# Three-stage attention and mixing kernel: weight conversion taken off GpSimd, wider weight pieces, more result buffers

## The chip, the core and the metric

The kernel runs on one core of a Trainium2 chip. The metric is the device time of one execution in microseconds (us); lower is better. In the text PE is the matrix engine (TensorE), PEld its weight loads, DVE is VectorE, ACT is ScalarE, POOL is GpSimd, and SP is the engine that here only issues transfers (DMAs). ACT issues some transfers too.

## The reference, cut to what matters

The batch is 4, the sequence 768, the model width 512. An attention block (not touched) gives `x`. Two mixing blocks follow:

```python
# channel mixing: the end of block 2
y = yr + yi                       # token mixing with w_tok_r, w_tok_i
u = x + y
x = u + np.maximum(u @ w_ch, 0.0)
# gated block 3
h = gelu(x @ w_in)                # w_in is 512 x 1024: u is the first half, v the second
u, v = h[..., :512], h[..., 512:]
v_n = (v - mean(v)) / sqrt(var(v) + 1e-6) * g_ln
v_s = einsum('ts,bsd->btd', w_sg, v_n) + b_sg[None, :, None]
out = x + (u * v_s) @ w_out
```

Some inputs (`w_theta`, `w_ch`, `w_in`, `w_out` and the token weights) come in float64, `w_sg` in float32. The kernel keeps every weight as a pair of float32r tiles, high and low, and does each product as three matmuls (high*high, high*low, low*high).

## The kernel before, in words

**Stages.** PE walks through the program in a fixed order. First comes attention with the theta products (line 311, tile `th`) and the token mixing (line 378), up to 382.6 us of the profile. A theta product of one unit (12 matmuls) is followed by 24 matmuls of token mixing; `th` has one buffer in PSUM, and the next theta product can start when DVE's line 325 has read it. When a set of units is complete, DVE adds up `u` (lines 388, 389) and SP stores it to DRAM.

Then comes channel mixing, function `chan(c, e)`: 8 slices `c` of `u`, each with 4 groups `e` of 12 matmuls (line 432). DVE makes the result `x2e` of a group from PSUM (line 438), and SP stores it to DRAM. Each slice needs `uhi` (ACT) and `ulo` (DVE, line 113), which `split_u` makes from `uf`, loaded back from DRAM.

Then comes the gated stage, for each of four batch entries `b`: `h_v` (6 groups, line 514, with a gelu on ACT in line 520 that gives `gv`, and statistics on DVE), `rstd`, `h_u` (8 groups, line 552), `norm`, `v_s` (line 577), `final` (line 597). Only `b = 0` has weight conversions beside it.

PE's groups take their PSUM tile from four `acc` buffers: a group can start when the reader of the group four places before it is done.

**Weight conversion.** Class `Weights` loads a piece with a DMA into a `raw` buffer, and `convert` makes the two tiles from it. For a float64 piece the steps are: line 150 on ACT (`cvh`), lines 153, 156 and 160 on DVE (`cvh`, `cvm`), line 203 on ACT (the high tile), line 204 on DVE, then line 208 (`cvh` minus high) and line 209 (plus `cvm`: the low tile). Before the change lines 208 and 209 run on POOL for `w_ch`, `w_in` and `w_out`. A piece was 256 columns wide (256 KB) in `w_ch`, `w_in` and `w_out`, 384 columns in `w_sg`. `w_sg` is float32 and needs only a cast on ACT and a subtraction on DVE (both in line 112 or 113). The `raw` buffer of a float64 piece is free once DVE's line 204 has run.

`w_ch` is converted late in token mixing (from 319 us of the profile), `w_in` during channel mixing, `w_sg` and `w_out` around the end of channel mixing and in the first `h_v` and `h_u`. The loads of the gated stage's weights are issued by ACT, all other loads and stores in this part by SP.

**What sets the order.** The program is written with tile pools; a scheduler puts the instructions of each engine into one fixed order when the kernel is built, and each engine runs its own list strictly in that order. An instruction that waits holds up everything behind it on its engine.

Of the kernel before, what the change touches and what calls it, by code (L numbers as in the profile page):

```python
# [8 lines left out]
I32 = mybir.dt.int32  # L9
# [7 lines left out]
B, H, S, D = 4, 8, 768, 64  # L17
DM = H * D
# [14 lines left out]
def net_kernel(tc, qt, kw, vw, ident, w_theta, w_tok, w_ch, w_in, w_sg, w_out, g_ln, b_sg, out):  # L33
    nc = tc.nc

    def opened(name, bufs=1, **kw_):
        cm = tc.tile_pool(name=name, bufs=bufs, **kw_)
        return cm, cm.__enter__()

    NRAW = 3  # L40
    AO, CO = -4, -2
    NRAW1, NCV1 = 3, 2
    ZB = 2
# [71 lines left out]
    class Weights:  # L115
# [1 line left out]

        def __init__(self, pool, pieces, nraw, ncv=2, queue=None, raws=()):  # L120
            self.queue, self.raws = queue or nc.sync, raws
            self.pool, self.pieces, self.raw = pool, pieces, {}
            self.nraw, self.ncv = nraw, ncv
            self.n = max(p[0].shape[-1] for p in pieces if p[0].dtype != F32)

        def load(self, j):
# [17 lines left out]
        def bits(self, raw, n, scale, mag="act", rem="dve"):  # L144

            words = raw[:, 0:2 * n].rearrange("p (n t) -> p n t", t=2)
            low, high = words[:, :, 0], words[:, :, 1]
            h = self.pool.tile([128, self.n], I32, tag="cvh", name="cvh", bufs=self.ncv)[:, 0:n]
            m = self.pool.tile([128, self.n], I32, tag="cvm", name="cvm", bufs=self.ncv)[:, 0:n]
            nc.scalar.activation(  # L150
                out=h.bitcast(F32), in_=high.bitcast(F32), func=AF.Copy, scale=REBIAS
            )
            nc.vector.tensor_scalar(
                out=h, in0=h, scalar1=3, scalar2=None, op0=ALU.logical_shift_left
            )
# [239 lines left out]
    p2 = {}  # L395
# [50 lines left out]
    def open_w3():  # L446
        p3["w_cm"], w = opened("w3")
        p3["in_hi"] = [w.tile([128, KD, FF], F32R, name=f"in_hi{i}") for i in range(2)]
        p3["in_lo"] = [w.tile([128, KD, FF], F32R, name=f"in_lo{i}") for i in range(2)]
        p3["sg_hi"] = [w.tile([128, 2, S], F32R, name=f"sg_hi{i}") for i in range(3)]  # L450
        p3["sg_lo"] = [w.tile([128, 2, S], F32R, name=f"sg_lo{i}") for i in range(3)]
        p3["out_hi"] = w.tile([128, KD, DM], F32R, name="out_hi")
        p3["out_lo"] = w.tile([128, KD, DM], F32R, name="out_lo")
        p3["b"] = w.tile([128, S], F32, name="b_bc")
        p3["g"] = w.tile([128, KD], F32, name="g_col")
        open_x3()
        p3["s_cm"], stg3 = opened("stg3", bufs=2)
        pieces = []
        for j in (1, 0):
            for k in range(KD):  # L460
                for i, c in enumerate((slice(0, 256), slice(256, 512))):
                    pieces.append((
                        w_in[j, k, i], p3["in_hi"][j][:, k, c], p3["in_lo"][j][:, k, c]
                    ))
        for s in range(NBLK):
            for i, c in enumerate((slice(0, TC), slice(TC, S))):
                pieces.append((
                    w_sg[s, i],
                    p3["sg_hi"][s // 2][:, s % 2, c], p3["sg_lo"][s // 2][:, s % 2, c],
                ))  # L470
        for k in range(KD):
            for i, c in enumerate((slice(0, 256), slice(256, 512))):
                pieces.append((w_out[k, i], p3["out_hi"][:, k, c], p3["out_lo"][:, k, c]))
        p3["w"] = Weights(stg3, pieces, NRAW, 2, nc.scalar)
        nc.sync.dma_start(out=p3["b"], in_=b_sg.unsqueeze(0).to_broadcast([128, S]))
        nc.sync.dma_start(out=p3["g"], in_=g_ln)

# [127 lines left out]


    NU = len(units)
    half = dict(sub="pool", add="pool")
    P2, P3, P4 = [half], [dict(add="pool")], [half]
    NA = B * NBLK  # L610


# [32 lines left out]
    if True:  # L645
# [85 lines left out]
        for it in range(NU):  # L731
            run(it, -2)
            run(it, -1)
            for q in range(4):
                if has_theta(it + 2) and q == (3 if it < NBLK else 0):
                    theta(it + 2)
                run(it, q)
                if it >= 0:
                    mix_group(it, q)
                if it < CO + NFIRST and q == 3:  # L740
                    tok_conv()
                if last_att + 2 <= it < last_att + 6 and q % 2:
                    j = 2 * (it - last_att - 2) + q // 2
                    p2["w"].convert(j, **half)
                    p2["w"].load(j + NRAW)
                if has_theta(it + 2) and q == 3:
                    z_split(it + 2)
            run(it, 9)
            if it == NFIRST + CO - 1:
                close(st_cm)  # L750
                s1_cm, set1 = opened("set1")
                sets[1] = x_set(set1, 1, None)
            if it == last_att + 1:
                close(at_cm)
                close(s0_cm)
                open_p2()
                load_u(0)
                load_u(1)
                load_u(2)
            if it == last_att + 6:  # L760
                split_u(0)
        close(s1_cm)
        close(wk_cm)
        close(w1_cm)
        p2["x_cm"], p2["x"] = opened("p2x", bufs=2, side="right")
        open_w3()
# [25 lines left out]
        for b in range(B):  # L792
            for s in range(NBLK):
                h_v(b, s)
                if b == 0:
                    for _ in range(2):
                        w3s.convert(jw, **P3[jw % len(P3)])
                        w3s.load(jw + NRAW)
                        jw += 1
            rstd()  # L800
            for c in range(2):
                for f in range(KD):
                    h_u(b, c, f)
                    if b == 0:
                        w3s.convert(jw, **P4[jw % len(P4)])
                        w3s.load(jw + NRAW)
                        jw += 1
                    if c == 0:
                        norm(f)
                    elif f < 2:  # L810
                        norm(4 + f)
            if b == 0:
                close(p3["s_cm"])
            p3["xr"] = [x3_t.pop(2 * b), x3_t.pop(2 * b + 1)]
            if b + 1 < B:
                load_x2(2 * b + 2)
            for c in range(2):
                for f in range(KD):
                    v_s(b, c, f)
            if b + 1 < B:  # L820
                split_x2(2 * b + 2)
            for e in range(KD):
                final(b, 0, e)
            if b + 1 < B:
                load_x2(2 * b + 3)
                split_x2(2 * b + 3)
            for e in range(KD):
                final(b, 1, e)
# [4 lines left out]
def _layout(inp):  # L833
# [26 lines left out]
    def pieces(w, n):  # L860

        w = w.reshape(w.shape[0] // 128, 128, w.shape[1] // n, n).transpose(0, 2, 1, 3)
        return np.ascontiguousarray(w)
# [41 lines left out]
```

## Time and profile before

| | before |
|---|---|
| median of 3 runs | 769.97 us (769.75 to 771.89) |
| the profiled execution's own time | 770.49 us |
| its span in the profile | 768.7 us |
| PE busy | 732.5 us (95% of the span) |
| DVE busy | 495.0 us (64%) |
| ACT busy | 311.2 us (40%) |
| POOL busy | 61.3 us (8%), 64 of its 70 instructions are lines 208 and 209 |

Busy time is the union of an engine's instructions. Matmuls overlap on PE, so a matmul's duration in a row is longer than the distance from its start to the next one's. 1.8 us lie between the span and the execution's own time.

### The profile page before, as it was taken

Reading aid. Unit: us, or ns where it says so; the run is one execution under the profiler, and the core shown is the slowest. Engines: PE = TensorE matmul, PEld = TensorE weight load, DVE = VectorE, ACT = ScalarE, POOL = GpSimd, SP = SyncE. Lnnn points to the kernel's source line nnn. Section 1 sums busy time; section 2 is a strip of 40 time slices with the busy share of each in tenths; the row PEclk is TensorE's granted clock in tenths of the full one; section 3 lists DMA queues with packets and bytes.
Section 4 is the critical chain, followed back from the end, with each engine's and each line's share of the span. In section 5 each row is a group of like instructions: output and inputs, shape, how many; then the busy total and the mean of one; then the engine's idle time right before and its main releaser. Section 6 shows DMA issues by size and latency. Waiting matters only on the chain.

```text
span 768.7 us, 16388 instructions
## 1 busy us (share of the span) xinstructions
PE 732.5 (95%) x6968; PEld 680.8 (89%) x6968; DVE 495.0 (64%) x934; ACT 311.2 (40%) x500; POOL 61.3 (8%) x70
## 2 busy tenths in 40 slices
PE   5979999999999999989998899899999999999998
PEld 3757888999999999989997897899899989998998
DVE  5999898667476665896478958853355435543452
ACT  5965534545545545452124334711151125113310
POOL 0000000000000000160045614200000000000000
PEclk9998999999999999999999999999999999999999
DMA  9775376333233230521077865002100310030002
GB/s 343 283 236 176 134 227 193 111 99 129 95 126 123 84 128 2 205 71 42 28 248 255 285 194 152 10 1 103 62 1 1 109 57 1 1 113 10 1 1 83
DMA packets 35642, 86.92 MB, mean 113 GB/s; under 512 B 4081, under 2 KB 18033, under 8 KB 35569
## 3 DMA queue, kind: packets, MB, share of 16 engines
q1 hardware_dynamic: 30384, 77.22, 29.6%
q10 hardware_dynamic: 5184, 8.65, 4.0%
q8 instruction: 55, 0.90, 0.5%
q14 instruction: 19, 0.15, 0.1%
HBM read 66.98 MB, written 18.87 MB: 112 GB/s over the span
## 4 chain that ended last, share of the span: by engine, by line
PE 65%; DVE 18%; DMA 7%; ACT 6%; issue 3%; POOL 0%; SPq 0%; ACTq 0%; DVEq 0%; POOLq 0%
PE acc L378 16%; PE acc L577 13%; PE acc L597 9%; PE acc L552 8%; PE acc L514 7%; PE th L311 7%; PE att L234 3%; DVE cvh L156 2%; DVE cvm L204 2%; DMA raw<-w_sg 2%; DVE z L336 1%; DMA raw<-w_in 1%; DVE cvm L160 1%; PE att L258 1%; PE att L284 1%
## 5 line engine op out<-in xcount | busy, mean ns | idle before, releaser
L378 PE MATMUL acc<-tok,slot 128*128 128x384 f32 x552 | 116.9, 342 | 2.7 <-ACT slot L348 2.5
L378 PE MATMUL acc<-slot 128*128 128x384 f32 x552 | 115.6, 340 | 0.3 <-DVE u L388 0.3
L378 PEld LDWEIGHTS acc<-tok,slot 128*128 128x128 f32 x552 | 94.5, 188 | 5.2 <-ACT slot L348 2.8
L378 PEld LDWEIGHTS acc<-slot 128*128 128x128 f32 x552 | 95.5, 188 | 2.3 <-DVE u L388 0.6
L577 PE MATMUL acc<-sg_hi,vlo 128*128 128x384 f32 x192 | 64.4, 336 | 0.0
L577 PE MATMUL acc<-sg_hi,vhi 128*128 128x384 f32 x192 | 64.4, 336 | 0.0
L577 PE MATMUL acc<-sg_lo,vhi 128*128 128x384 f32 x192 | 64.4, 336 | 0.0
L311 PE MATMUL th<-th_hi,xhi 128*128 128x256 f32 (+1 forms) x168 | 53.1, 316 | 4.2 <-DVE slot_x L325 2.6
L112 ACT ACTIVATE ghi<-g 128x384 fp32r<-128x384 f32 x32 | 16.8, 525 | 87.7 <-DVE g L586 87.7
L311 PE MATMUL th<-th_hi,xlo 128*128 128x256 f32 (+1 forms) x168 | 51.6, 307 | 0.2 <-DVE xlo L113 0.2
L582 DVE SCALAR_TENSOR_TENSOR g<-acc,g_col,b_bc 128x384 f32<-128x384 f32 x32 | 19.8, 618 | 49.5 <-PE acc L577 49.5
L311 PE MATMUL th<-th_lo,xhi 128*128 128x256 f32 (+1 forms) x168 | 50.8, 302 | 0.0
L432 PE MATMUL acc<-uhi,ch_hi 128*128 128x384 f32 x128 | 44.7, 349 | 5.8 <-DVE x2e L438 5.6
L150 ACT ACTIVATE cvh<-raw 128x256 f32<-128x256 f32 (+1 forms) x44 | 24.8, 564 | 56.6 <-DMA raw<-w_in 19.9
L552 PE MATMUL acc<-x3hi,in_hi 128*128 128x384 f32 x128 | 43.2, 337 | 2.1 <-ACT gu L557 1.3
L432 PE MATMUL acc<-ulo,ch_hi 128*128 128x384 f32 x128 | 44.1, 344 | 0.5 <-DVE ulo L113 0.5
L432 PE MATMUL acc<-uhi,ch_lo 128*128 128x384 f32 x128 | 43.9, 343 | 0.0
L552 PE MATMUL acc<-x3lo,in_hi 128*128 128x384 f32 x128 | 43.0, 336 | 0.0
L552 PE MATMUL acc<-x3hi,in_lo 128*128 128x384 f32 x128 | 43.0, 336 | 0.0
L597 PE MATMUL acc<-glo,out_hi 128*128 128x384 f32 x128 | 43.0, 336 | 0.0
L597 PE MATMUL acc<-ghi,out_lo 128*128 128x384 f32 x128 | 42.9, 335 | 0.0
L597 PE MATMUL acc<-ghi,out_hi 128*128 128x384 f32 x128 | 42.9, 335 | 0.0
(141 smaller groups left out, 1627.5 us busy)
## 6 DMA issues: line engine op xcount, KB each, us to landing
va<-vw SPq DMA_DIRECT2D x24, 520.0 KB, 4.0
ka<-kw SPq DMA_DIRECT2D x24, 512.0 KB, 4.6
raw<-w_tok SPq DMA_DIRECT2D x12, 768.0 KB, 5.7
q<-qt SPq DMA_DIRECT2D x24, 256.0 KB, 3.0
u_dram<-u SPq DMA_DIRECT2D x32, 192.0 KB, 2.2
uf<-u_dram SPq DMA_DIRECT2D x8, 768.0 KB, 6.8
x_dram<-x2e SPq DMA_DIRECT2D x32, 192.0 KB, 3.3
x3f<-x_dram SPq DMA_DIRECT2D x8, 768.0 KB, 4.8
```

The source lines that it names most:

```text
L112: nc.scalar.activation(out=hi, in_=src, func=AF.Copy)
L150: nc.scalar.activation(out=h.bitcast(F32), in_=high.bitcast(F32), func=AF.Copy, scale=REBIAS)
L156: nc.vector.scalar_tensor_tensor(out=h, in0=high, scalar=-0x80000000, in1=h, op0=ALU.bitwise_and, op1=ALU.bitwise_or,)
L234: nc.tensor.matmul(out=out[32 * c:32 * c + 32, j, n * a:n * a + n], lhsT=lhs[h, a, 32 * c:32 * c + 32], rhs=rhs[h, 4 * a + c, :], start=Tr ...
L311: nc.tensor.matmul(out=th, lhsT=a[:, k, tok], rhs=w[:, k, cols], start=(i == 0), stop=(i == 3 * KD - 1),)
L378: nc.tensor.matmul(out=acc[:, 0:TC], lhsT=z[ri][:, zc], rhs=w[:, ri], start=(first and i == 0), stop=(last and i == 5),)
L432: nc.tensor.matmul(out=acc[:, 0:TC], lhsT=w[:, k, ee], rhs=x[:, k, :], start=(i == 0), stop=(i == 3 * KD - 1),)
L514: nc.tensor.matmul(out=acc, lhsT=x[:, k, tt], rhs=w[:, k, :], start=(i == 0), stop=(i == 3 * KD - 1),)
L552: nc.tensor.matmul(out=acc[:, 0:TC], lhsT=w[:, k, ff], rhs=x[:, k, :], start=(i == 0), stop=(i == 3 * KD - 1),)
L577: nc.tensor.matmul(out=acc[:, 0:TC], lhsT=v, rhs=w, start=(i == 0), stop=(i == 3 * NBLK - 1))
L582: nc.vector.scalar_tensor_tensor(out=g, in0=acc[:, 0:TC], scalar=p3["g"][:, f:f + 1], in1=p3["b"][:, tt], op0=ALU.mult, op1=ALU.add,)
L597: nc.tensor.matmul(out=acc[:, 0:TC], lhsT=w[:, k, ee], rhs=x[:, k, :], start=(i == 0), stop=(i == 3 * KD - 1),)
```

## The change

Three things are edited.

1. `w_ch`, `w_in` and `w_out` are converted with lines 208 and 209 on DVE in place of POOL.
2. The pieces of the gated stage's weights are twice as wide: `w_in` and `w_out` 512 columns (512 KB), `w_sg` 768 columns. There are half as many of them (8, 6 and 4), two `raw` buffers in place of three, and one `cvm` buffer in place of two. In `chan`'s loop a piece of `w_in` is converted at `e` 1 and 3 of the first two slices and at `e` 1 of the next four.
3. The pool of `x2e` has four buffers in place of two.

```diff
-    NRAW = 3
+    NRAW, NRAW3 = 3, 2
...
-            m = self.pool.tile([128, self.n], I32, tag="cvm", name="cvm", bufs=self.ncv)[:, 0:n]
+            m = self.pool.tile([128, self.n], I32, tag="cvm", name="cvm", bufs=self.ncm)[:, 0:n]
...
         for j in (1, 0):
             for k in range(KD):
-                for i, c in enumerate((slice(0, 256), slice(256, 512))):
-                    pieces.append((
-                        w_in[j, k, i], p3["in_hi"][j][:, k, c], p3["in_lo"][j][:, k, c]
-                    ))
+                pieces.append((w_in[j, k], p3["in_hi"][j][:, k], p3["in_lo"][j][:, k]))
...
-        p3["w"] = Weights(stg3, pieces, NRAW, 2, nc.scalar)
+        p3["w"] = Weights(stg3, pieces, NRAW3, 2, nc.scalar, ncm=1)
...
-    half = dict(sub="pool", add="pool")
-    P2, P3, P4 = [half], [dict(add="pool")], [half]
...
-                    p2["w"].convert(j, **half)
+                    p2["w"].convert(j)
...
-        p2["x_cm"], p2["x"] = opened("p2x", bufs=2, side="right")
+        p2["x_cm"], p2["x"] = opened("p2x", bufs=4, side="right")
...
-                if (e in (1, 3) or c < 2) and c < 7 and jw < 4 * KD:
-                    w3s.convert(jw, **P2[jw % len(P2)])
-                    w3s.load(jw + NRAW)
+                if (e == 1 or c < 2 and e == 3) and jw < 2 * KD:
+                    w3s.convert(jw)
+                    w3s.load(jw + NRAW3)
                     jw += 1
...
             for s in range(NBLK):
                 h_v(b, s)
                 if b == 0:
-                    for _ in range(2):
-                        w3s.convert(jw, **P3[jw % len(P3)])
-                        w3s.load(jw + NRAW)
-                        jw += 1
+                    w3s.convert(jw)
+                    w3s.load(jw + NRAW3)
+                    jw += 1
...
-                    if b == 0:
-                        w3s.convert(jw, **P4[jw % len(P4)])
-                        w3s.load(jw + NRAW)
+                    if b == 0 and f % 2:
+                        w3s.convert(jw)
+                        w3s.load(jw + NRAW3)
                         jw += 1
```

PE's list keeps its order. The lists of DVE and ACT change at three places that matter below.

**DVE late in token mixing.** The theta product here is `th_4435`, and `ulo_5091` (before) is the `ulo` of slice 1 of channel mixing. Before:

```order
L113 TENSOR_TENSOR ulo_4776<-uf_4429,uhi_4775 128x1536
L113 TENSOR_TENSOR slot_1875<-z_4385,slot_1875 128x512
L322 TENSOR_SCALAR slot_x_2018<-th_4435 128x256
L113 TENSOR_TENSOR ulo_5091<-uf_4431,uhi_5090 128x1536
L325 TENSOR_TENSOR slot_x_2018<-th_4435,slot_x_2018 128x256
```

With the change:

```order
L113 TENSOR_TENSOR ulo_4776<-uf_4429,uhi_4775 128x1536
L113 TENSOR_TENSOR slot_1875<-z_4385,slot_1875 128x512
L322 TENSOR_SCALAR slot_x_2018<-th_4435 128x256
L160 TENSOR_SCALAR cvm_4538<-cvh_4537 128x256
L325 TENSOR_TENSOR slot_x_2018<-th_4435,slot_x_2018 128x256
L204 SCALAR_TENSOR_TENSOR cvm_4538<-raw_4427,cvm_4538 128x256
L331 TENSOR_SCALAR z_4450<-slot_x_2018 128x256
L208 TENSOR_TENSOR cvh_4537<-cvh_4537,ch_hi_4421 128x256
```

The second `ulo` no longer stands between lines 322 and 325; it comes after line 325 of the next theta product, and lines 208 and 209 of `w_ch` are now in this list.

**DVE in channel mixing.** `x2e_5205` and `x2e_5237` are the results of groups 6 and 7 (of 0 to 31) before; `cvh_5180` is the sixth half-width piece of `w_in`. Before:

```order
L438 SCALAR_TENSOR_TENSOR x2e_5205<-acc_5192,uf_4431 128x384
L160 TENSOR_SCALAR cvm_5153<-cvh_5152 128x256
L204 SCALAR_TENSOR_TENSOR cvm_5153<-raw_5072,cvm_5153 128x256
L153 TENSOR_SCALAR cvh_5180<-cvh_5180 128x256
L156 SCALAR_TENSOR_TENSOR cvh_5180<-raw_5104,cvh_5180 128x256
L438 SCALAR_TENSOR_TENSOR x2e_5237<-acc_5224,uf_4431 128x384
```

With the change `x2e_5187` and `x2e_5217` are the results of groups 7 and 8, and `cvh_5142` and `cvh_5190` are the third and fourth full-width pieces:

```order
L438 SCALAR_TENSOR_TENSOR x2e_5187<-acc_5174,uf_4431 128x384
L160 TENSOR_SCALAR cvm_5143<-cvh_5142 128x512
L113 TENSOR_TENSOR ulo_5265<-uf_5108,uhi_5264 128x1536
L204 SCALAR_TENSOR_TENSOR cvm_5143<-raw_5058,cvm_5143 128x512
L208 TENSOR_TENSOR cvh_5142<-cvh_5142,in_hi1_4991 128x512
L153 TENSOR_SCALAR cvh_5190<-cvh_5190 128x512
L209 TENSOR_TENSOR in_lo1_4993<-cvh_5142,cvm_5143 128x512
L156 SCALAR_TENSOR_TENSOR cvh_5190<-raw_5106,cvh_5190 128x512
L438 SCALAR_TENSOR_TENSOR x2e_5217<-acc_5204,uf_4433 128x384
```

In both lists a line 153 that needs a piece's data stands ahead of a result that PE waits for; with the change it is a full-width piece, with lines 208 and 209 of the piece before it beside it.

**ACT at the start of the gated stage.** `gv0` is the gelu of the first `h_v` group; `raw_5923` and so on are pieces of `w_out`. Before:

```order
L112 ACTIVATE sg_hi2_4996<-raw_5919 128x384
L150 ACTIVATE cvh_5969<-raw_5923 128x256
L139 DMA raw_5947<-w_out 128x512
L150 ACTIVATE cvh_5998<-raw_5943 128x256
L203 ACTIVATE out_hi_5000<-cvh_5969 128x256
L139 DMA raw_5979<-w_out 128x512
L203 ACTIVATE out_hi_5000<-cvh_5998 128x256
L150 ACTIVATE cvh_6027<-raw_5947 128x256
L139 DMA raw_6008<-w_out 128x512
L520 ACT_TABLE_LOAD
L520 ACTIVATE gv0_5778<-acc_5805 128x512
```

With the change (line 512 is line 520 of before):

```order
L112 ACTIVATE sg_hi2_4996<-raw_5765 128x768
L112 ACTIVATE sg_hi2_4996<-raw_5785 128x768
L139 DMA raw_5805<-w_out 128x1024
L512 ACT_TABLE_LOAD
L512 ACTIVATE gv0_5680<-acc_5707 128x512
L139 DMA raw_5825<-w_out 128x1024
L512 ACTIVATE gv1_5681<-acc_5727 128x512
```

Three casts of `w_out` pieces and two of its high tiles no longer stand ahead of the first gelu.

## Rows read from the trace of the kernel before

**Rows 1.** Stretches: us; busy PE, PEld, DVE, ACT, POOL; PE clock; DMA share; GB/s.

```profile
316.00:382.60 66.60, 63.41 (x395) 62.12 (x394) 47.73 (x97) 24.00 (x48) 15.52 (x16) 1.00 0.25 86
382.60:460.50 77.90, 71.61 (x387) 68.95 (x386) 61.34 (x114) 27.80 (x49) 32.68 (x32) 0.96 0.75 244
460.50:498.40 37.90, 34.35 (x169) 30.10 (x169) 31.96 (x68) 22.43 (x43) 12.79 (x16) 1.00 0.31 87
540.00:573.50 33.50, 33.50 (x171) 30.23 (x170) 15.23 (x32) 14.16 (x23) 0.00 (x0) 1.00 0.09 32
```

**Rows 2.** PE's waits from 316 to 500 us: total, times, longest.

```profile
PE acc L432 <- DVE x2e L438: 5.6, 5, 2.2
PE th L311 <- DVE slot_x L325: 2.6, 2, 1.6
```

**Rows 3.** PE around a wait in channel mixing: start, duration, idle before.

```profile
405.18 0.33 PE L432 MATMUL acc<-uhi,ch_lo 128*128 128x384 f32 x1
405.35 0.34 PE L432 MATMUL acc<-ulo,ch_hi 128*128 128x384 f32 x1
407.60 0.44 PE L432 MATMUL acc<-uhi,ch_hi 128*128 128x384 f32 x1 [1.91 <-DVE x2e L438]
...
409.52 0.52 PE L432 MATMUL acc<-uhi,ch_hi 128*128 128x384 f32 x1
409.84 0.52 PE L432 MATMUL acc<-uhi,ch_lo 128*128 128x384 f32 x1
```

**Rows 4.** DVE at the same place.

```profile
406.32 0.29 DVE L153 TENSOR_SCALAR cvh<-cvh 128x256 int32<-128x256 int32 x1 [2.69 <-ACT cvh L150]
406.65 0.42 DVE L156 SCALAR_TENSOR_TENSOR cvh<-raw,cvh 128x256 int32<-128x256 int32 x1
406.99 0.55 DVE L438 SCALAR_TENSOR_TENSOR x2e<-acc,uf 128x384 f32<-128x384 f32 x1
```

**Rows 5.** The chain that ended last, at the same place: start, length, what.

```profile
399.57 6.21 DMA raw<-w_in
```

**Rows 6.** DMA issues of the whole span: KB each, median us to landing.

```profile
ka<-kw SPq DMA_DIRECT2D x24, 512.0 KB, 4.6
...
raw<-w_in ACTq DMA_DIRECT2D x16, 256.0 KB, 3.6
```

**Rows 7.** Instruction groups by shape: busy us, mean ns of one, idle before.

```profile
L156 DVE SCALAR_TENSOR_TENSOR cvh<-raw,cvh 128x256 int32<-128x256 int32 x32 | 19.9, 624 | 0.4
...
L208 POOL TENSOR_TENSOR cvh<-cvh,in_hi 128x256 f32<-128x256 f32 x16 | 18.0, 1129 | 66.2 <-ACT in_hi L203 50.4 <-DVE cvm L160 13.0 <-DVE cvh L153 1.7
...
L438 DVE SCALAR_TENSOR_TENSOR x2e<-acc,uf 128x384 f32<-128x384 f32 x32 | 17.4, 549 | 2.3 <-PE acc L432 1.3 <-DMA x_dram<-x2e 0.8
...
L113 DVE TENSOR_TENSOR vlo<-gv,vhi 128x512 fp32r<-128x512 f32 x24 | 15.5, 685 | 0.2 <-ACT vhi L112 0.2
...
L113 DVE TENSOR_TENSOR x3lo<-x3f,x3hi 128x1536 fp32r<-128x1536 f32 x8 | 14.0, 1755 | 2.4 <-ACT x3hi L112 2.4
...
L176 DVE SCALAR_TENSOR_TENSOR th_lo<-slot,cvm 128x512 fp32r<-128x512 uint32 x4 | 2.8, 690 | 0.1
L156 DVE SCALAR_TENSOR_TENSOR cvh<-slot,cvh 128x512 int32<-128x512 int32 x4 | 2.7, 687 | 0.1
L150 ACT ACTIVATE cvh<-slot 128x512 f32<-128x512 f32 x4 | 2.7, 671 | 5.1 <-DMA slot<-w_theta 5.0
...
L153 DVE TENSOR_SCALAR cvh<-cvh 128x512 int32<-128x512 int32 x4 | 1.7, 423 | 1.9 <-ACT cvh L150 1.8
```

**Rows 8.** DVE, then PE, at a wait in token mixing.

```profile
330.24 1.96 DVE L113 TENSOR_TENSOR ulo<-uf,uhi 128x1536 fp32r<-128x1536 f32 x1
...
332.58 0.38 PE L311 MATMUL th<-th_hi,xhi 128*128 128x256 f32 x1 [1.57 <-DVE slot_x L325]
```

**Rows 9.** ACT at the start of the gated stage.

```profile
464.09 0.52 ACT L112 ACTIVATE sg_hi<-raw 128x384 fp32r<-128x384 f32 x1 [1.00 <-DVE sg_lo L113]
...
471.38 1.28 ACT L520 ACT_TABLE_LOAD   x1 [0.39 <-ACT cvh L150]
```

More of the change, by code (lines that the diff above doesn't have):

```diff
@@ L115, in net_kernel, with __init__ @@
     class Weights:
-        def __init__(self, pool, pieces, nraw, ncv=2, queue=None, raws=()):
+        def __init__(self, pool, pieces, nraw, ncv=2, queue=None, raws=(), ncm=None):
             self.queue, self.raws = queue or nc.sync, raws
             self.pool, self.pieces, self.raw = pool, pieces, {}
-            self.nraw, self.ncv = nraw, ncv
+            self.nraw, self.ncv, self.ncm = nraw, ncv, ncm or ncv
             self.n = max(p[0].shape[-1] for p in pieces if p[0].dtype != F32)
@@ L460, in open_w3 @@
             for k in range(KD):
-                for i, c in enumerate((slice(0, 256), slice(256, 512))):
-                    pieces.append((
-                        w_in[j, k, i], p3["in_hi"][j][:, k, c], p3["in_lo"][j][:, k, c]
-                    ))
+                pieces.append((w_in[j, k], p3["in_hi"][j][:, k], p3["in_lo"][j][:, k]))
         for s in range(NBLK):
[L466 to L470, printed above, removed]
+            pieces.append((w_sg[s], p3["sg_hi"][s // 2][:, s % 2], p3["sg_lo"][s // 2][:, s % 2]))
         for k in range(KD):
-            for i, c in enumerate((slice(0, 256), slice(256, 512))):
-                pieces.append((w_out[k, i], p3["out_hi"][:, k, c], p3["out_lo"][:, k, c]))
-        p3["w"] = Weights(stg3, pieces, NRAW, 2, nc.scalar)
+            pieces.append((w_out[k], p3["out_hi"][:, k], p3["out_lo"][:, k]))
+        p3["w"] = Weights(stg3, pieces, NRAW3, 2, nc.scalar, ncm=1)
         nc.sync.dma_start(out=p3["b"], in_=b_sg.unsqueeze(0).to_broadcast([128, S]))
@@ L764, in net_kernel @@
         close(w1_cm)
-        p2["x_cm"], p2["x"] = opened("p2x", bufs=2, side="right")
+        p2["x_cm"], p2["x"] = opened("p2x", bufs=4, side="right")
         open_w3()
         w3s = p3["w"]
-        for j in range(NRAW):
+        for j in range(NRAW3):
             w3s.load(j)
@@ L875, in _layout @@
         "w_ch": pieces(inp["moe_w_ch"], 256),
-        "w_in": np.stack([pieces(w_in[:, :FF], 256), pieces(w_in[:, FF:], 256)]),
-        "w_sg": pieces(inp["moe2_w_sg"].T, TC),
-        "w_out": pieces(inp["moe2_w_out"], 256),
+        "w_in": np.stack([pieces(w_in[:, :FF], FF)[:, 0], pieces(w_in[:, FF:], FF)[:, 0]]),
+        "w_sg": pieces(inp["moe2_w_sg"].T, S)[:, 0],
+        "w_out": pieces(inp["moe2_w_out"], DM)[:, 0],
         "g_ln": np.ascontiguousarray(inp["moe2_g_ln"].reshape(KD, 128).T),
```

## The prediction

> **What bounds the kernel now.** I first read the busy shares of the page's head (the table above): PE is busy 95% of the span, so the end is set by PE's list and by the moments in which PE stands still. Since the change leaves PE's work alone, it can only win or lose such moments. Then I cut the span at the stages [rows 1]. In the second half of token mixing PE is idle 66.6 - 63.4 = 3.2 us. Channel mixing takes 77.9 us. Its 384 matmuls start 0.17 us apart when nothing stops them (405.18 and 405.35 in [rows 3]; over longer runs 0.1735), which is 66.6 us, so 11.3 us are lost there. The first `h_v` and `h_u` take 37.9 us, the same work for `b = 1` 33.5 us [rows 1], so 4.4 us are lost there. After it, and from `b = 1` on, PE has no gap. At most 3.2 + 11.3 + 4.4 = 18.9 us can be won.
>
> Then the waits. In channel mixing PE waits for `x2e` on DVE [rows 2]. The place at 407.60 shows how: PE stops for 1.91 us [rows 3]; DVE's line 438 that frees its PSUM tile starts at 406.99, right behind a line 153 that had stood still for 2.69 us because ACT's cast had no data [rows 4]; the data came by a transfer that took 6.21 us [rows 5], where the median is 3.6 [rows 6]. So it is not DVE's load alone: DVE waits in order for a weight piece while the result that PE needs stands behind it. The wait costs twice: at 409.52 the matmuls start 0.32 us apart, not 0.17 [rows 3]. The granted clock over the stage is 0.96 [rows 1]; if the rest of it ran at 2.4 GHz, some 6.2 us (2 x 0.04 x 77.9) ran at 1.2 GHz, in which about 19 matmuls fit and not 36: 2.9 us of the 11.3 are the clock after waits. I count 1.4 us for each of two long waits.
>
> **The change, part by part.**
>
> Lines 208 and 209 on DVE. The 64 POOL instructions go; the 1129 ns of one [rows 7] was latency inside a conversion, not on PE's path. What also goes is DVE's slowing beside POOL: line 156 took 0.42 us alone [rows 4] and 0.624 on average [rows 7]. What DVE gains: in token mixing 16 instructions of 256 columns at about 0.42 us (the price of line 156, which reads two SBUF tiles too), 6.7 us. Against it stand four lines for each of eight pieces that get back between 0 and 0.2 us each, 0 to 6.4. DVE is busy 47.7 of 66.6 us there [rows 1], so this may lie beside other work. What matters is the order: before, line 325 stood behind an `ulo` of 1.96 us, and PE waited 1.57 us at 332.58 [rows 8], 2.6 in two such places [rows 2]. After, line 325 follows line 160 at once; by durations it ends about 0.5 us before PE wants it at the first place, and about 1 us before at the next three. The last term of the 3.2 us, some 0.5 us around the `u` additions, stays. I take a gain of 2.5 us. Bounds: 2.7 won, or 1.5 lost if one 6.7 us lump lands before a line 325 with only that 0.5 us of room.
>
> Wide pieces in channel mixing. One piece costs DVE 0.42 + 0.69 + 0.42 + 0.69 + 2 x 0.685 = 3.6 us (lines 153, 156, 160 at line 153's price, 204 at line 176's, 208 and 209 at the price of `vlo`) [rows 7], less some 0.08 us for each overlap with the next. Two half pieces cost DVE 2 x (4 lines of 0.3 to 0.6), about the same, and then POOL. So DVE's total does not grow; the question is again what stands ahead of `x2e`.
>
> Count from the first matmul of channel mixing (time 0; group k is due at 2.08 k and needs the `x2e` of group k-4). Pieces 0 and 1 are issued at 2.5 as now, and land at 7 to 9. From line 153 of piece 0 (about 8.5) to the `x2e` of group 8 DVE has 4 lines 153, 4 of 156, 3 of 160, 3 of 204, 6 of 208 and 209, two `ulo` of 1.755 and six `x2e` of 0.55 [rows 7]: 18.7 us, less 27 overlaps of 0.08, makes 16.6: it would end at 25.1, just when group 12 is due (25.0). But line 153 of piece 3 must wait. Its buffer is free when line 204 of piece 1 has run (about 17), a 768 KB load of `x3f` is issued just before it, and it lands some 7 us later (a 512 KB load takes 4.6 [rows 6], a half piece with such loads ahead took 6.21 [rows 5]): 24. Then come the cast (0.67), line 153, line 209, line 156 and `x2e`: 26.9. PE stops for 1.9 us, and the clock costs 1.4. Piece 4 has the same fate: its load stands on ACT's list behind the `x3hi` cast, is issued at about 26.5, lands at 31.5, and the `x2e` of group 10 behind it ends at 34.6, when group 14 is due at 32.4: 2.2 us and 1.4 again. From piece 5 on fewer results stand between pieces, and DVE has room; I leave 1.1 us for late `ulo`. Sum 1.9 + 1.4 + 2.2 + 1.4 + 1.1 = 8.0 us lost, where 11.3 were: a gain of 3.3. Bounds: with all pieces in time nothing is lost (11.3 won); if pieces 2 to 7 each come 2 us later than I take, each stops PE for up to 2 us more: 12 more lost, 8.7 worse than now.
>
> A rule of the Trainium skill speaks to this. In the trace the half piece issued by ACT at 399.57 took 6.21 us [rows 5], as if it stood behind the larger loads on SP's queue. By the Trainium skill, "DMA: Bandwidth & Descriptors", section on queues, rings and completion order, each DMA engine takes turns between the queues that have work, packet by packet, so a small piece on ACT's queue should pass a large load on SP's. By that rule pieces 3 and 4 would land about 2 us earlier and both long waits would be gone, a total of about 755 us. The row fits it badly, so I do not sum by it.
>
> Four `x2e` buffers. DVE waited 0.8 us in all for the store of an old `x2e` [rows 7]; this goes, inside the 3.3 us.
>
> The gated stage's start. Before, the last high tile of `w_sg` was made at 464.09, and the table load ahead of the first gelu came at 471.38 [rows 9], 10.9 us after `h_v` began, held by `w_out` casts that waited for their loads. PE reaches the fifth `h_v` group after 4 x 12 matmuls of 0.234 us ((33.5 - 96 x 0.1735) / 72, with the 33.5 of [rows 1]), 11.2 us, and needs the first gelu by then. After, only the six `w_sg` pieces stand ahead. Six pieces in two buffers, about 6 us a pair (3.6 for the load, a cast and a subtraction of 768 columns of about 1 us each), begun about 9 us before channel mixing ends because only then are `raw` and ACT free, leave the gelu at about 5.5 us after its end: in time. `w_out` then goes between gelus; the last one may hold the eighth group for a few tenths. I take 0.6 of 4.4 us lost, a gain of 3.8 (bounds: 0.5 if every `w_sg` pair takes 4 us more and the gelu is as late as now, 4.4).
>
> Sum: 2.5 + 3.3 + 3.8 = 9.6 us. The profiled execution had 770.49 us; 770.49 - 9.6 = 760.9. The median of the runs is 0.5 us lower: 769.97 - 9.6 = 760.4 us. Changes under 0.3% (2.3 us) can't be told from none.
>
> **The rivals.**
>
> *Loads in time (0.18).* The waits for pieces 3 and 4 go, since wider loads need fewer turn-arounds. For: 3.6 us is the median for a piece [rows 6]. Against: the stage's DMA share of 0.75 [rows 1], which stays. Gain 2.5 + 7 to 11.3 + 4: 752 to 756 us.
>
> *The gain of channel mixing is eaten (0.20).* Pieces 3 to 6 stop PE as long as now, 11.3 us, and the clock with it; only the other two terms stay, one of them partly: 763.7 us, to 769 if both fall to half and channel mixing loses 2 more.
>
> *Two buffers are too few (0.09): slower.* With two buffers a pair of pieces costs a load of 7, a cast and 2.2 us of DVE, about 10 us, so pieces 2 to 7 take 30 us, and between their first and last lines stand the results of groups 6 to 20, 31 us of PE: just enough. If a pair took 17 us (a landing of 14), PE would be held to 51 us there: 20 lost, clock aside, for the 11.3 of now, against 6.3 won elsewhere: 772 us. It decides from a pair of about 16 us on. Against: no row near that size here.
>
> **How the numbers follow.** My forecast (756 to 763.5) gets 0.53, the rivals 0.18, 0.20 and 0.09. The range 752 to 768 leaves out the slower case, the worst of the second rival and the best of the first, about 0.2. Faster by over 0.3%: 0.53 + 0.18 + 0.12 of the second rival = 0.83. Within 0.3%: 0.09. Slower: 0.08.
>
> **What would show it.** Right: no POOL work beyond setup; line 156 at 0.69 us for 512 columns; no PE wait at line 311 for line 325 from 316 to 350; channel mixing in 72 to 76 us with one or two waits of about 2 us for `x2e`, behind a line 153 that waits for a piece, around groups 12 and 14, and the low clock after them; the first gelu some 6 us after `h_v` begins, `h_v` and `h_u` of `b = 0` in 34 us. Wrong: PE waits at other groups, or a channel mixing near 67 or above 78 us; DVE's instructions at 512 columns longer than 0.7 us; a new wait in token mixing.

## The result, and the profile after

The changed kernel takes 760.13 us (median of four executions, 757.85 to 762.43), the kernel before 770.12 (four, 769.75 to 771.89) beside it: a ratio of 0.986, with a 95% interval from 0.984 to 0.989, 10.0 us less. The prediction was 760.4. The profiled execution was the longest of the four, 762.43 us with a span of 760.6.

I cut the span at PE's first matmul of each stage. Ahead of them stands a fixed place that no edit touches, PE's wait at line 284 near 314 us; token mixing is counted from there. Lengths in us, with the change worked out:

| | before | after | change | predicted |
|---|---|---|---|---|
| up to the wait at line 284 | 313.60 | 315.30 | +1.7 | - |
| token mixing from there | 69.02 | 65.31 | -3.7 | -2.5 |
| channel mixing | 77.88 | 75.83 | -2.0 | -3.3 |
| `h_v` and `h_u` of `b = 0` | 37.94 | 33.75 | -4.2 | -3.8 |

The edited stages give 9.9 us; attention, which the change leaves alone, was 1.7 us longer in this execution. The stretches of the changed kernel that answer to [rows 1], the last 66.6 us of token mixing first, and two short ones inside channel mixing (the columns are those of [rows 1]):

```profile
314.00:380.60 66.60, 65.82 (x417) 65.21 (x416) 50.05 (x119) 24.30 (x49) 0.00 (x0) 1.00 0.26 92
380.60:456.44 75.84, 69.50 (x386) 67.98 (x385) 59.37 (x95) 25.01 (x28) 0.00 (x0) 0.98 0.75 255
456.44:490.19 33.75, 33.75 (x170) 30.49 (x169) 28.34 (x58) 21.49 (x34) 0.00 (x0) 1.00 0.28 88
414.00:424.00 10.00, 9.49 (x55) 9.17 (x55) 5.65 (x9) 1.56 (x3) 0.00 (x0) 1.00 0.98 335
...
430.00:440.00 10.00, 9.87 (x48) 9.87 (x49) 9.56 (x16) 3.53 (x4) 0.00 (x0) 0.83 0.59 198
```

POOL does nothing in them. The first `h_v` and `h_u` run without a gap, as `b = 1` did before. What is left of PE's waits from 316 to 500 us (total, times, longest), the answer to [rows 2]:

```profile
PE acc L432 <- DVE ulo L113: 4.1, 2, 3.6
PE acc L432 <- DVE x2e L438: 2.3, 2, 1.8
PE th L311 <- DVE slot_x L325: 0.3, 1, 0.3
```

The waits for `x2e` have shrunk from 5.6 us and a new one has come, for `ulo`. On PE (compare [rows 3]):

```profile
405.64 0.34 PE L432 MATMUL acc<-ulo,ch_hi 128*128 128x384 f32 x1
407.74 0.41 PE L432 MATMUL acc<-uhi,ch_hi 128*128 128x384 f32 x1 [1.76 <-DVE x2e L438]
407.99 0.34 PE L432 MATMUL acc<-uhi,ch_lo 128*128 128x384 f32 x1
...
426.22 0.34 PE L432 MATMUL acc<-uhi,ch_lo 128*128 128x384 f32 x1
430.13 0.54 PE L432 MATMUL acc<-ulo,ch_hi 128*128 128x384 f32 x1 [3.57 <-DVE ulo L113]
430.47 0.52 PE L432 MATMUL acc<-uhi,ch_hi 128*128 128x384 f32 x1
430.79 0.52 PE L432 MATMUL acc<-uhi,ch_lo 128*128 128x384 f32 x1
```

The first is matmul 144 of the stage, so group 12. After it the matmuls go on 0.17 us apart. The second is matmul 242, in group 20. After it eleven matmuls start 0.32 to 0.34 us apart, the lower of the two clock levels, which costs another 1.6 us. DVE at this second place (compare [rows 4]):

```profile
424.15 0.43 DVE L153 TENSOR_SCALAR cvh<-cvh 128x512 int32<-128x512 int32 x1 [4.50 <-ACT cvh L150]
...
428.32 1.75 DVE L113 TENSOR_TENSOR ulo<-uf,uhi 128x1536 fp32r<-128x1536 f32 x1
```

It is the picture of [rows 4] again, with another victim: a line 153 waits 4.5 us for a piece (piece 6, counted from 0), and the `ulo` that PE needs stands behind it, with seven instructions between. Two things make the piece late. Its load needs one of the two `raw` buffers, and is issued 0.09 us after DVE's line 204 of piece 4 has ended and freed one (DVE, then ACT's queue):

```profile
413.30 0.68 DVE L204 SCALAR_TENSOR_TENSOR cvm<-raw,cvm 128x512 f32<-128x512 uint32 x1
414.07 0.33 ACTq L139 DMA_DIRECT2D raw<-w_in  x1
```

Then the load takes 9.30 us, in the chain that ended last (start, length, what; it answers to [rows 5]):

```profile
414.07 9.30 DMA raw<-w_in
...
424.02 1.48 ACT uhi L112
...
428.40 1.68 DVE ulo L113
```

The transfers issued from 413 to 420 us (KB each, median us to landing; compare [rows 6]):

```profile
uf<-u_dram SPq DMA_DIRECT2D x2, 768.0 KB, 9.4
...
x3f<-x_dram SPq DMA_DIRECT2D x1, 768.0 KB, 8.6
raw<-w_in ACTq DMA_DIRECT2D x1, 512.0 KB, 9.3
```

From 414 to 424 us the DMA share is 0.98, and between 416.49 and 423.20 us none of the stage's transfers lands. Last, DVE in token mixing, where [rows 8] had an `ulo` ahead of line 325:

```profile
330.51 0.42 DVE L322 TENSOR_SCALAR slot_x<-th 128x256 f32<-128x256 f32 x1
330.85 0.28 DVE L160 TENSOR_SCALAR cvm<-cvh 128x256 int32<-128x256 int32 x1
331.05 0.42 DVE L325 TENSOR_TENSOR slot_x<-th,slot_x 128x256 f32<-128x256 f32 x1
```

### The profile page after: what moved, and what is told of

Its sections match the earlier page's. It is cut to its first block, busy times and chain, and to the rows that moved or that the text cites. A ratio compares the mean times of both kernels' runs of the same rounds, so it can differ in the third digit from the quotient of the medians.

```text
span 760.6 us, 16131 instructions
## 1 busy us (share of the span) xinstructions
PE 730.4 (96%) x6968; PEld 680.7 (89%) x6968; DVE 488.0 (64%) x920; ACT 306.9 (40%) x470; POOL 0.3 (0%) x6
## 4 chain that ended last, share of the span: by engine, by line
PE 70%; DVE 17%; DMA 6%; ACT 4%; issue 2%; SPq 0%; DVEq 0%; ACTq 0%
PE acc L378 15%; PE acc L569 13%; PE acc L506 9%; PE acc L544 9%; PE acc L589 9%; PE th L311 7%; PE acc L432 3%; PE att L234 3%; DMA raw<-w_in 2%; DVE cvh L156 2%; DVE cvh L208 1%; DVE z L336 1%; PE att L258 1%; DVE cvm L204 1%; DVE u L389 1%
## 5 line engine op out<-in xcount | busy, mean ns | idle before, releaser
L595 DVE TENSOR_TENSOR o<-acc,x3f 128x384 f32<-128x384 f32 x32 | 17.8, 555 | 37.3 <-PE acc L589 37.3
```

The lines of the kernel that those rows point to most:

```text
L595: nc.vector.tensor_tensor(out=o, in0=acc[:, 0:TC], in1=p3["xr"][c][:, e, :], op=ALU.add)
```

## The experiments

Each run stands beside runs of the kernel before on the same chip, so ratios are compared (95% interval in brackets). The lengths of the stages come from each kernel's one trace, cut as above:

| run | median us | ratio | token | channel | `h_v`, `h_u` | first gelu after |
|---|---|---|---|---|---|---|
| before | 770.12 | 1 | 69.0 | 77.9 | 37.9 | 12.2 |
| changed kernel | 760.13 | 0.986 [0.984, 0.989] | 65.3 | 75.8 | 33.8 | 6.1 |
| e1_wch_dve | 768.35 | 0.996 [0.993, 0.998] | 64.9 | 78.0 | 37.6 | 11.9 |
| e2_wch_pool | 762.23 | 0.989 [0.985, 0.993] | 68.7 | 74.9 | 33.8 | 5.8 |
| e3_x2_two | 766.59 | 0.994 [0.992, 0.997] | 65.1 | 80.6 | 33.8 | 9.1 |
| e4_wide_pool | 770.12 | 0.999 [0.997, 1.001] | 64.9 | 83.6 | 34.7 | 11.7 |
| e5_again | 759.29 | 0.983 [0.980, 0.986] | 65.3 | 76.4 | 33.8 | 5.5 |
| e6_narrow_x4 | 763.0 | 0.988 [0.986, 0.991] | 65.3 | 76.9 | 33.8 | 6.2 |
| e7_before_x4 | 771.46 | 0.999 [0.997, 1.001] | 69.2 | 79.4 | 37.8 | 13.2 |
| e8_pool_idle | 763.09 | 0.989 [0.986, 0.991] | 65.1 | 77.0 | 33.8 | 8.8 |
| e9_x3_late | 759.67 | 0.985 [0.982, 0.988] | 64.9 | 76.0 | 33.8 | 9.4 |
| e10_split_early | 758.14 | 0.983 [0.981, 0.986] | 64.7 | 70.8 | 33.8 | 9.4 |
| e11_both | 758.5 | 0.983 [0.981, 0.986] | 65.0 | 69.3 | 34.6 | 10.9 |
| e12_early_six | 757.17 | 0.982 [0.980, 0.985] | 65.1 | 70.8 | 34.2 | 9.8 |

The last column is the start of the first gelu, counted from the first `h_v` matmul.

**One term alone, and all but one.** Two runs ask whether the three terms of the sum are separate.

```diff
 # e1_wch_dve: the kernel before
-                    p2["w"].convert(j, **half)
+                    p2["w"].convert(j)
 # e2_wch_pool: the changed kernel
-                    p2["w"].convert(j)
+                    p2["w"].convert(j, sub="pool", add="pool")
```

> The kernel before, with lines 208 and 209 of w_ch alone on DVE; gated weights and x2e as before. My sum (three separate terms): only the token-mixing term shows, token mixing 2.5 to 3.7 us shorter, channel mixing 77.9 and the first h_v and h_u 37.9 as before, so 766.3 to 767.6 us. Rival 'one cause' (DVE freed of waiting beside POOL, and the stages after it start with DVE ahead): the later stages get shorter too, 763 us or less. Rival 'chance of the one profile': token mixing as before, 770.

> The changed kernel, with lines 208 and 209 of w_ch back on POOL; gated weights and four x2e buffers as changed. My sum: token mixing goes back to about 69 us with the waits of line 311 for line 325, the rest stays, so 3 to 3.7 us more than the changed kernel, 763 to 764 us. Rival 'one cause': all terms hang on it, 766 us or more. Rival 'chance': no difference, 760.

The term of token mixing is separate from the other two. e1 shortens token mixing by 4.1 us and leaves the later stages as they were; it is 0.45% faster, 3.5 us. e2's trace gives token mixing back and keeps the rest; its time alone, with a ratio of 0.989 against 0.986, would not tell it from the changed kernel. The wait is the one of [rows 2]:

```profile
PE th L311 <- DVE slot_x L325: 2.4, 2, 1.4
```

**Two `x2e` buffers.**

```diff
-        p2["x_cm"], p2["x"] = opened("p2x", bufs=4, side="right")
+        p2["x_cm"], p2["x"] = opened("p2x", bufs=2, side="right")
```

> The changed kernel with two buffers for x2e, not four. My sum: four buffers were worth the 0.8 us that DVE waited for a store before, hidden for the most part, so 760 to 761 us. Rival 'the buffers are the change': in channel mixing DVE stands at x2e until a store has landed, PE behind it, and channel mixing goes back to 78 us or more: 762 us or more. With a DMA share of 0.7 to 0.8 a store's landing could take as long as the pieces' did.

The rival was right, and my price for this edit wrong: 766.59 us, and channel mixing takes 80.6. `h_v` and `h_u` stay at 33.8 us, so these two terms are separate too. DVE's waits in channel mixing say what happens (0.8 us of this kind in the whole kernel before, [rows 7]):

```profile
DVE x2e L438 <- DMA x_dram<-x2e: 12.1, 7, 5.4
```

The reverse run, four buffers in the kernel before, gives nothing:

```diff
-        p2["x_cm"], p2["x"] = opened("p2x", bufs=2, side="right")
+        p2["x_cm"], p2["x"] = opened("p2x", bufs=4, side="right")
```

> The kernel before with four buffers for x2e as the only edit. My prediction had them at no more than the 0.8 us that DVE waited for a store, hidden in part: 769.3 to 770.5, the same within the measurement. Rival, after the run of the changed kernel with two buffers (766.6, some 6 us more than with four): the buffers carry a gain by themselves, 764 to 767 us. Between them: they only count once DVE does the conversions alone and reaches x2e sooner.

Here it was the prediction's price that held (ratio 0.999). So the buffers are worth nothing with the old conversions, and 0.8 to 1.1% (6 to 9 us by the ratios) with the new ones. Not all of that need be the waits: in e3 the lists of DVE and ACT come in another order too. Why the new conversions need the buffers stays open. It is not simply slower stores: their median landing in channel mixing is 3.3 us before, 3.8 in e3, 4.0 with the narrow pieces of e6 and 4.1 in the changed kernel.

**POOL, with wide pieces.**

```diff
+    def wide3(j):
+        return p3["w"].pieces[j][0].dtype != F32
...
-                    w3s.convert(jw)
+                    w3s.convert(jw, add="pool", sub="pool" if wide3(jw) else "dve")
```

> The changed kernel, with lines 208 and 209 of the wide gated pieces (512 columns) on POOL; w_ch on DVE. By the rows of before (1129 ns for one of 256 columns) two of 512 take POOL 4 to 4.5 us a piece, and DVE's own lines beside it get longer (line 156 took 0.624 for 256 columns beside POOL, 0.42 alone). My theory: a piece's latency grows from 3.6 to some 6 us, but DVE has 1.4 us a piece less to do, so x2e stands behind less: channel mixing 75 to 80 us, the gelu later by some 3 us: 760 to 766. Rival 'POOL is what cost the time': channel mixing 78 or more and the first h_v and h_u at 37 or more, 766 to 770. Rival 'width is what won it': no difference from the changed kernel within 2 us.

It loses the whole gain: 770.12 us, with a channel mixing 5.7 us longer than in the kernel before. DVE's own lines beside POOL in its channel mixing (1.75 and 0.68 us in the changed kernel), and ACT between its groups 14 and 16 and at the first gelu:

```profile
L113 DVE TENSOR_TENSOR ulo<-uf,uhi 128x1536 fp32r<-128x1536 f32 x6 | 12.7, 2120 | 1.8 <-ACT uhi L112 1.7
L156 DVE SCALAR_TENSOR_TENSOR cvh<-raw,cvh 128x512 int32<-128x512 int32 x9 | 8.7, 966 | 0.1
```

```profile
414.15 1.48 ACT L112 ACTIVATE x3hi<-x3f 128x1536 fp32r<-128x1536 f32 x1 [6.25 <-DMA x3f<-x_dram]
...
468.84 0.66 ACT L150 ACTIVATE cvh<-raw 128x512 f32<-128x512 f32 x1 [1.56 <-DMA raw<-w_out]
472.61 1.28 ACT L512 ACT_TABLE_LOAD   x1 [3.10 <-DMA x_dram<-x2e]
```

Two things at once: DVE's lines get longer (by a fifth and by four tenths here), and the order is another one. On ACT an `x3hi` that waits 6.25 us for its load stands ahead of the next piece's load and of `uhi`, and casts of `w_out` stand ahead of the gelu again. The next run takes the first alone.

```diff
+            if self.ncm == 1 and j < 2 * KD:
+                idle = p2["x"].tile([128, self.n], F32, tag="idle", name="idle", bufs=1)
+                for _ in range(2):
+                    nc.gpsimd.tensor_tensor(out=idle, in0=r32(hi), in1=r32(hi), op=ALU.add)
```

> The changed kernel, with two POOL additions of 128x512 f32 beside every w_in conversion whose result nothing reads. Nothing waits for POOL here. Theory 'DVE slows beside POOL': lines 156, 204, 153 and ulo get 1.4 to 1.7 times as long where they overlap, 4 to 5 us of POOL a piece, so DVE needs some 8 to 11 us more in channel mixing, which gets 2 to 6 us longer: 762 to 766 us. Rival 'the round trip through POOL is what cost the run with wide pieces on POOL 10 us': no difference, 760 us.

DVE in its channel mixing (line 212 is line 208 of the others):

```profile
L212 DVE TENSOR_TENSOR cvh<-cvh,in_hi 128x512 f32<-128x512 f32 x8 | 10.5, 1315 | 0.1
L204 DVE SCALAR_TENSOR_TENSOR cvm<-raw,cvm 128x512 f32<-128x512 uint32 x8 | 8.9, 1116 | 0.0
L156 DVE SCALAR_TENSOR_TENSOR cvh<-raw,cvh 128x512 int32<-128x512 int32 x8 | 6.3, 785 | 0.0
```

DVE's list is that of the changed kernel, and POOL work for which nobody waits costs some 3 to 4 us of the 10 that e4 loses (763.09 us, by the medians; its trace, of the shortest execution of the set, shows 0.6 to 1.2 of that in channel mixing). Lines 208, 204 and 156, with two operands in SBUF, take 1315, 1116 and 785 ns where they took 684, 683 and 682. The Trainium skill, "SBUF — State Buffer", section "Who interferes with whom", says that a DVE instruction with two SBUF inputs contends with a GpSimd instruction that reads SBUF; the trace agrees. Line 160, which has one, went from 419 to 520 ns as well. The other 6 to 7 us of e4 go with the new order and POOL's longer way; these two I did not part.

**The change without the wider pieces.** All conversions on DVE, pieces of 256 columns with three buffers, four `x2e` buffers.

```diff
 # the kernel before
-    half = dict(sub="pool", add="pool")
-    P2, P3, P4 = [half], [dict(add="pool")], [half]
+    half = dict()
+    P2, P3, P4 = [half], [dict()], [half]
...
-        p2["x_cm"], p2["x"] = opened("p2x", bufs=2, side="right")
+        p2["x_cm"], p2["x"] = opened("p2x", bufs=4, side="right")
```

> The change without the wider pieces: all of lines 208 and 209 on DVE, gated weights in 256 columns with three buffers as before, four buffers for x2e. By my prediction width itself gives DVE nothing (3.6 us a piece either way), but the w_out casts would again stand ahead of the first gelu: token mixing 65, channel mixing 75 to 77, h_v and h_u 37.5: 763.5 to 766 us. Rival 'width won channel mixing' (fewer turn-arounds of a load): channel mixing 79 or more, 767 us or more. Rival 'width is nothing': 760 us.

763.0 us, but not where I put it: channel mixing is 0.5 to 1.1 us longer than with wide pieces, and the gated stage starts without a gap. ACT there, with narrow pieces:

```profile
463.66 1.28 ACT L520 ACT_TABLE_LOAD   x1
464.27 0.33 ACTq L139 DMA_DIRECT2D raw<-w_out  x1
```

and in the changed kernel (compare [rows 9]):

```profile
460.17 0.34 ACTq L139 DMA_DIRECT2D raw<-w_out  x1
461.25 1.28 ACT L512 ACT_TABLE_LOAD   x1 [0.30 <-DMA x_dram<-x2e]
```

In both no cast of `w_out` stands ahead of the gelu. So the width did not make this order. By the last column of the table the engine matters: with lines 208 and 209 of the gated weights on POOL (before, e1, e4, e7) three or four casts of `w_out` stand ahead of the gelu, and it starts 11.7 to 13.2 us after `h_v` in either width; with them on DVE it starts at 5.5 to 10.9 us, and PE waits 0.2 us at most for it. But the engine is not all: e3, on DVE with two `x2e` buffers, has two such casts ahead of it (9.1 us), e9 and e11, with the held loads, one. What width is worth is not well fixed: 0.2 to 0.5% by the ratios (1 to 4 us), of which this one trace shows 0.5 to 1.1 in channel mixing.

**Is the wait for `ulo` an accident?** The changed kernel again, unedited.

> The changed kernel once more, unedited, for a second trace and a closer time. My theory: the 3.6 us for which PE stood at 430 us of the first trace came from transfers that took 9.3 us in that execution and is no fixed part; another execution has it shorter or elsewhere, and the time lies between 757.5 and 762.5 us, median 760. Rival: the wait is built into the order, stands at the same matmul with 3 us or more in every trace; then the runs' spread of 4.6 us has another cause.

It is no accident, though at 2.9 us the wait is just under the 3 that the rival asked for. It stands at the same matmul, 242, and again `uf` and a piece take 8.8 us there:

```profile
PE acc L432 <- DVE ulo L113: 3.5, 2, 2.9
```

Built into the order it is not. In e8, with the same list on DVE, PE had lost more time ahead of that matmul and came to it 6 us later:

```profile
430.12 0.44 PE L436 MATMUL acc<-ulo,ch_hi 128*128 128x384 f32 x1 [0.31 <-DVE ulo L113]
```

**Transfers or order?** Two edits take one each.

```diff
 # e9_x3_late
-    def load_x2(c):
+    def load_x2(c, gate=None):
         x = p3["x"].tile([128, KD, TC], F32, tag="x3f", name="x3f", bufs=3)
+        if gate is not None:
+            nc.gpsimd.tensor_copy(out=x[:, 0, 0:1], in_=r32(us_t[gate][0][:, 0, 0:1]))
...
-                load_x2(0)
-                load_x2(1)
+                load_x2(0, 6)
+                load_x2(1, 6)
...
-                load_x2(2 * b + 2)
+                load_x2(2 * b + 2, 7 if b == 0 else None)
 # e10_split_early
-                if e == 2 and c + 1 < NC2:
+                if e == 1 and c + 1 < NC2:
                     split_u(c + 1)
```

> The changed kernel, with the first three loads of x3f (768 KB each, read first at the end of channel mixing, the third only for b = 1) held back until the uhi of slice 6 (third: slice 7) exists, by a copy of one column on POOL into the tile. Same work. Theory 'the transfers stand in each other's way' (in two traces uf and a piece issued near 413 took 8.8 to 9.4 us at a DMA share of 0.96 to 0.98, with x3f among them): uf and pieces land in 4 to 7 us there, PE's wait for ulo 49 to 50 us into channel mixing (2.9 and 3.6 us in two traces) falls under 1.5, channel mixing is 3 to 6 us shorter: 754 to 757 us. Rival 'the order on DVE' (ulo stands behind lines 153 to 156 of a piece whatever lands): 759 to 760 us.

> The changed kernel with the split of the next u slice one chan call earlier (ahead of the conversion of the same slice, not behind it); loads as changed. Theory 'the order on DVE': ulo of slice 5 no longer stands behind a line 153 that waits for a piece, the wait of 2.9 to 3.6 us and the low clock after it go: 755 to 757 us. Rival 'the transfers': uf of slice 5 lands at 421.6 to 423.2 whatever, ulo can start 3 us earlier at most, and other results stand behind it: 758 to 760 us.

With `x3f` out of the way the landings in that place fall to these, from 9.4 and 9.3 us:

```profile
uf<-u_dram SPq DMA_DIRECT2D x2, 768.0 KB, 6.1
...
raw<-w_in ACTq DMA_DIRECT2D x1, 512.0 KB, 7.0
```

and the wait for `ulo` falls to 1.6 us. But channel mixing is as long as in the changed kernel (76.0 us), since the held load now delays something else. DVE, then PE:

```profile
447.65 1.76 DVE L113 TENSOR_TENSOR x3lo<-x3f,x3hi 128x1536 fp32r<-128x1536 f32 x1 [3.77 <-ACT x3hi L112]
449.32 1.01 DVE L438 SCALAR_TENSOR_TENSOR x2e<-acc,uf 128x384 f32<-128x384 f32 x2
```

```profile
449.93 0.44 PE L432 MATMUL acc<-uhi,ch_hi 128*128 128x384 f32 x1 [1.87 <-DVE x2e L438]
```

The theory of the transfers was right about the landings and wrong about the gain. With the split earlier the wait is gone and the trace's channel mixing is 5 to 5.5 us shorter. That is not the order alone: in e10 this `uf` and this piece landed in 6.5 us each, where they took 9.4 and 9.3, with an `x3f` still issued beside them; why, the rows do not say. The three traces together part the two. PE starts matmul 241 at 45.6 to 45.8 us of the stage in each, and matmul 242 at 49.5 in the changed kernel, at 47.5 in e9 (landings of 6.2 and 7.0 us, `ulo` behind as before) and at 45.95 in e10 (6.5 and 6.5, `ulo` ahead). So sooner landings took 2.0 us of that wait, and the order the last 1.6. DVE at the same place now, `ulo` ahead of a line 153 that waits:

```profile
421.02 1.75 DVE L113 TENSOR_TENSOR ulo<-uf,uhi 128x1536 fp32r<-128x1536 f32 x1
...
426.90 0.43 DVE L153 TENSOR_SCALAR cvh<-cvh 128x512 int32<-128x512 int32 x1 [1.67 <-ACT cvh L150]
```

**Both, and a second look.**

> Both edits of the two runs before: x3f late and the split earlier. If the transfers are the cause, the second edit adds nothing to the first, within 1 us; if both count, their gains add: 752 to 756 us. Channel mixing can't get below 66.6 us, 8.5 to 9 us less than in the changed kernel, so 751 us is the floor of this.

```diff
 # e12_early_six: e10 and
-        p2["x_cm"], p2["x"] = opened("p2x", bufs=4, side="right")
+        p2["x_cm"], p2["x"] = opened("p2x", bufs=6, side="right")
```

> The split one chan call earlier, and six buffers for x2e where there were four; the order of DVE's instructions is that of the run with the split earlier alone. Its trace took 70.8 us for channel mixing with no wait for ulo over 0.4 us, in an execution of 754.3, but its median was 758.1. If the order took the wait away for good, this trace has again no wait for ulo over 1 us about 50 us into channel mixing, and channel mixing in 70 to 72.5 us; the two more buffers end the 1.1 us that DVE waited for a store, hidden in part: median 756.5 to 758.5. Rival 'that trace was a lucky execution': the wait of 2 us or more is back there, channel mixing at 74 or more, 758 to 760.5 us.

e11's channel mixing is the shortest, 69.3 us (66.6 is all matmuls). e12 confirms e10: 70.8 us, no wait for `ulo` over 0.8 us:

```profile
PE acc L432 <- DVE x2e L438: 1.9, 2, 1.6
PE acc L432 <- DVE ulo L113: 1.2, 2, 0.8
```

The times are another matter. e10's median, 758.14, lies in the range of its rival, and e11's 758.5 outside its own 752 to 756. 758.1, 758.5 and 757.2 us against 759.3 and 760.1 of the changed kernel are 1 to 3 us less, and the ratios (0.982 to 0.983 against 0.983 to 0.986) can't tell them apart. The traces promise 5. Both traces of the changed kernel come from the longest execution of their set (762.43 and 760.77; the seven others average 758.9), e10's from its shortest (754.3). e10's five others average 758.5. So either the changed kernel's executions without a profile lose less at `ulo` than its traces show, or e10's lose more than its trace; their stages can't be seen, and this stays open. Three `raw` buffers for the wide pieces were not tried.

## Why the prediction was right, point by point

**Token mixing** (2.5 us): right in mechanism, too small, and outside its bound of 2.7: 3.7 us, 4.1 in e1. Line 325 follows line 160 at 331.05, and PE's waits for it fell from 2.6 to 0.3 us. One mistake is in the base: I took PE's idle time, 3.2 us, as all there was to win. But a matmul's record covers the start of the next one, so idle time leaves out some 0.2 us for each wait. By the distances from start to start the gaps of over 0.6 us cost 4.0 us before (1.8 and 1.3 for line 325, two of 0.44 for line 388) and 0.5 after. The other is the term that was to stay, the two waits around the `u` additions (line 388): they went too, and with them 0.9 of the 3.7 us; why, no run asks.

**Channel mixing** (8.0 us lost; 11.3 before): 9.2 were lost, so the gain is 2.0 us (1.5 in e5), not 3.3. The first wait stood in the group named, 12, behind the line 153 of a piece, and cost 1.93 us for the 1.9 predicted. The low clock after it did not come in this trace; in e5 the wait there was 2.3 us, and it came. The second, in group 14, was 0.7 us and not 2.2: piece 4's load stood ahead of the `x3hi` cast in ACT's list, not behind it, was issued at 24.4 us of the stage and not at 26.5, and landed at 29.2 and not at 31.5. So the two waits that were summed cost less than said, and the step that failed is "From piece 5 on fewer results stand between pieces, and DVE has room": in group 20 PE lost 3.7 us and 1.6 more to the clock, behind piece 6. I had counted what stands between two pieces on DVE, but took 5 to 7 us for a landing; with `uf`, `x3f`, the piece and five stores sharing the DMA engines at a share of 0.98 it took 9.3, and the `ulo` that PE needed stood behind that piece's line 153. By e9 and e10 both had a part in that wait, the late landing and the order. That the stage came near the forecast is in part luck: two waits and the clock after them taken too large, against one wait not foreseen.

By the Trainium skill, "DMA: Bandwidth & Descriptors", section "Queues, rings and completion order", DMA engines take turns between queues. What I had drawn from it and did not sum by, that a piece on ACT's queue passes the larger loads on SP's, did not show in the landings, which do not say whether the engines took turns: the piece on ACT's queue, issued 0.24 us after a `uf` on SP's, landed at 423.37 us, 0.17 us after the larger `uf` at 423.20.

**The wide pieces' price on DVE** (0.69 us for lines of two operands, 0.42 for the others) was right, and e8 shows that part of the old price was POOL:

```profile
L156 DVE SCALAR_TENSOR_TENSOR cvh<-raw,cvh 128x512 int32<-128x512 int32 x12 | 8.2, 682 | 0.1
...
L153 DVE TENSOR_SCALAR cvh<-cvh 128x512 int32<-128x512 int32 x16 | 6.7, 419 | 11.6 <-ACT cvh L150 11.6
...
L156 DVE SCALAR_TENSOR_TENSOR cvh<-raw,cvh 128x256 int32<-128x256 int32 x8 | 3.3, 417 | 0.0
```

**Four `x2e` buffers** ("0.8 us, inside") were mis-sized. The 0.8 us is what the old order waited; with the new conversions and two buffers DVE waits 12.1 us for stores, and e3 is 0.8 to 1.1% slower.

**The gated stage's start** (3.8 us): 4.2, the first gelu 6.1 us after `h_v` begins, where some 6 were named. The reason was half wrong: e6 has the same with narrow pieces, so the new order on ACT came with the engine of lines 208 and 209 and, by e3, the `x2e` buffers. And the first gelu is less than half of the term. Before, PE waited in this stage at three places:

```profile
PE acc L514 <- ACT gv L520: 1.5, 1, 1.5
PE acc L552 <- ACT gu L557: 1.3, 1, 1.3
PE acc L552 <- ACT gv L520: 0.8, 1, 0.8
```

From start to start the first, at the fifth group, cost 1.6 us, and the two in `h_u` 2.4. The prediction priced the 4.4 us lost as one, by the late first gelu, and not the later waits; they went as well.

**The sum** was 9.6 us and the edited stages gave 9.9: terms of 2.5, 3.3 and 3.8 became 3.7, 2.0 and 4.2. The first and the last were too small, the middle one too large, so the errors cancelled.

## What to carry to other kernels

Where an engine runs its list in order, look at every instruction that waits for a transfer and ask what result stands behind it: the long waits followed here in channel mixing were of that kind, first `x2e`, then `ulo`, then `x2e` behind `x3lo`. In the traces one call moved in the source was worth more there than the later loads were, though part of it came with sooner landings and the times do not show it. Price a buffer in the order that the change makes, not by the waits of the order before: the same two buffers were worth nothing and 6 us or more. And count a wait on PE from start to start, since overlapping records hide part of it.

## What the runs showed that I had not expected

PE's wait at line 284, ahead of everything that was edited, came at 312.8 to 316.5 us in the fourteen traces: a spread of nearly 4 us that no edit made. Stages have to be compared from such a mark on, not by the span. A wait of 1.76 us left the clock of the next matmuls at its higher level in one trace (407.74 us), and one of 2.92 us did so in e8, while one of 1.91 us was followed by matmuls 0.32 us apart in [rows 3]; so the length of the wait alone does not decide it, and the 1.4 us that the prediction put on each long wait are no fixed price. And PE's list did change at one place: in group 16 the first matmul that needs `ulo` comes two places later (matmul 196, not 194).
